# Three late stores of a decode-attention backward kernel go by rows in steps of 2, 4 and 8, and two small outputs leave in smaller pieces

## The chip, the cores and the metric

The kernel runs on one core of one Trainium2 chip. The metric is the device time of one execution in microseconds (us), the median of three runs. The profile is one further execution taken with the hardware profiler; its span runs from the first to the last instruction, and every position "at 714.57" in this text is in us from the start of that span.

## What is computed

The reference is one decode step (one token) of a transformer block, attention over a cache beside a gated MLP, and its gradients:

```python
def _A_ref(x, k_cache, v_cache, wq, wo):          # 32 heads, 8192 keys, head size 128
    q = (x @ wq).reshape(B, Sq, Hq, Dh).transpose(0, 2, 1, 3)
    scores = jnp.einsum("bhqd,bhkd->bhqk", q, k) * (Dh ** -0.5)
    p = _softmax(scores, axis=-1)
    o = jnp.einsum("bhqk,bhkd->bhqd", p, v)
    return o.transpose(0, 2, 1, 3).reshape(B, Sq, Hq * Dh) @ wo

def _B_ref(x, w1, w3, w2):
    h = _silu(x @ w1) * (x @ w3)
    return h @ w2

xn = _layernorm(A_x)
out = A_x + _A_ref(xn, ...) + _B_ref(xn, ...)
# returned: out, and the gradients of A_x, k_cache, v_cache, wq, wo, w1, w3, w2 for a given grad_out
```

All tensors are bf16. The two caches are 32 heads x 8192 x 128, which is 2 MB for each head; they are read once, and their gradients, of the same size, are written once. That is 64 loads and 64 stores of 2 MB. out_0 is the output row (640 numbers), out_1 the gradient of the input row (640 numbers), out_2 and out_3 the gradients of the K and V caches.

## The kernel before, where the change touches it

K and V of a head are loaded into one of ten buffers as 128 partitions (rows) of 16 KB each. The gradient of the head is written over the loaded data in place, and the buffer is stored from there. All these loads and stores go through one function, which issues them from SyncE in the order of the calls:

```python
dkc = out_2.rearrange("b h (p j) d -> (b h) p (j d)", p=P)     # P = 128
dvc = out_3.rearrange("b h (p j) d -> (b h) p (j d)", p=P)
...
def fifo(out_, in_):
    nc.sync.dma_start(out_, in_)
...
def load_next():
    if not pending or len(free_slots) < lag[0]:
        return
    kind, h = pending.pop(0)
    t = free_slots.pop(0)
    fifo(t[:], (kc if kind == "K" else vc)[h])
    kv_tiles[(kind, h)] = t
...
def store(kind, h):
    t = kv_tiles.pop((kind, h))
    if kind == "K":
        hd.pop(h)
    fifo((dkc if kind == "K" else dvc)[h], t[:])
    free_slots.append(t)
    load_next()
```

The gradients are outer products on VectorE (line 466). They and the stores run one head behind the forward part; the last head is finished after the loop, and the last weight gradients follow:

```python
def outers_a(h):
    outer_v(h, 0, J // 2)
    outer_v(h, J // 2, J)
    store("V", h)
    outer_k(h, 0, J // 2)

def outers_b(h):
    outer_k(h, J // 2, J)
    store("K", h)
...
outers_a(H - 1)                      # H = 32
outers_b(H - 1)
fin_od(NG - 1)
fin_pe(NG - 1)
fin_wo(NG - 1)                       # store of the wo gradient, issued from GpSimd
for ci in range(NC):
    fin_wq(NG - 1, ci)               # store of the wq gradient, issued from GpSimd
...
nc.vector.tensor_copy(row_bf, acc[:, 0:DHALF])
out_0v = out_0.rearrange("a b (e c) -> (a b e) c", e=2)
for e in range(2):
    nc.scalar.dma_start(out_0v[e:e + 1, :], row_bf[64 * e:64 * e + 1, :])
...                                  # layernorm gradient, some 10 small instructions
nc.vector.tensor_copy(fin_bf[:], ps_o[0:NC, 0:P])          # NC = 5
nc.scalar.dma_start(out_1.rearrange("a b (c p) -> (a b c) p", p=P), fin_bf[:])
```

The order of the last stores is therefore V29, K29, V30, K30, V31, K31 (heads count from 0). The tile framework gives each transfer issued from SyncE or ScalarE one of eight completion semaphores[...].

Of the kernel before, what the change touches and what calls it, by code (L numbers as in the profile page):

```python
# [16 lines left out]
P = 128  # L17
# [4 lines left out]
def kernel(  # L22
# [22 lines left out]
    nc = tc.nc  # L45
    H = A_k_cache.shape[1]
# [5 lines left out]
    NC = D // P  # L52
# [23 lines left out]
    dkc = out_2.rearrange("b h (p j) d -> (b h) p (j d)", p=P)  # L76
    dvc = out_3.rearrange("b h (p j) d -> (b h) p (j d)", p=P)
# [26 lines left out]
    def fifo(out_, in_):  # L104
        nc.sync.dma_start(out_, in_)
# [16 lines left out]
# [7 lines that stand above are left out]
# [84 lines left out]
    def t_tile():  # L213
        t = kt_tile()
        return t[:].rearrange("p k w -> p (k w)").bitcast(BF16)
# [248 lines left out]
    def outer(dst, vec, pair, lo, hi):  # L464
        n = hi - lo
        nc.vector.tensor_tensor(  # L466
            dst[:, lo * DH:hi * DH].rearrange("p (j a b) -> p j a b", a=DH // 2, b=2),
            vec.rearrange("p (a b) -> p a b", b=2).unsqueeze(1).to_broadcast([P, n, DH // 2, 2]),
            pair[:, lo:hi, :].unsqueeze(2).to_broadcast([P, n, DH // 2, 2]), ALU.mult)
# [4 lines left out]
    def outer_k(h, lo, hi):  # L474
        outer(kv_tiles[("K", h)], hd[h]["qd"][:, 0, :], hd[h]["U2"], lo, hi)

    def store(kind, h):
        t = kv_tiles.pop((kind, h))
        if kind == "K":
            hd.pop(h)  # L480
        fifo((dkc if kind == "K" else dvc)[h], t[:])
        free_slots.append(t)
        load_next()

# [236 lines left out]
# [9 lines that stand above are left out]
# [102 lines left out]
    nc.vector.tensor_tensor(dxn[:], dxn[:], dxm[:], ALU.add)  # L832
    row_bf = t_tile()[:, 0:DHALF]
    nc.vector.tensor_copy(row_bf, acc[:, 0:DHALF])
    out_0v = out_0.rearrange("a b (e c) -> (a b e) c", e=2)
    for e in range(2):
        nc.scalar.dma_start(out_0v[e:e + 1, :], row_bf[64 * e:64 * e + 1, :])
    st = consts.tile([P, 2], F32, name="st")
    nc.vector.tensor_reduce(st[:, 0:1], dxn[:], AX.X, ALU.add)
    junk5 = consts.tile([P, NC], F32, name="junk5")  # L840
# [10 lines left out]
    nc.tensor.transpose(ps_o[0:NC, 0:P], fin[:], ident_f[:])  # L851
    fin_bf = consts.tile([NC, P], BF16, name="fin_bf")
    nc.vector.tensor_copy(fin_bf[:], ps_o[0:NC, 0:P])
    nc.scalar.dma_start(out_1.rearrange("a b (c p) -> (a b c) p", p=P), fin_bf[:])


# [28 lines left out]
```

## Time and profile before

| what | value |
|---|---|
| time, median of 3 | 732.62 us (732.5 to 733.53) |
| profiled span | 731.1 us |
| moved by DMA | 303.53 MB, mean 415 GB/s |
| stores of K and V gradients | 64 of 2048 KB, 31.0 us from issue to landing |
| loads of K and V | 64 of 2048 KB, 26.3 us from issue to landing |
| TensorE, VectorE, ScalarE busy | 82%, 63%, 51% of the span |
| last load (V31) issued, landed | 660.35, 686.66 |
| last outer product (K31) ends | 706.1 |
| out_0 issued, out_1 issued | 714.57, 717.24 |

A line of the grouped views reads: source line, engine, operation, output<-input, count, then busy time. In a line of the timeline the first number is the start, the second how long it took. SPq and ACTq are the queues in which SyncE and ScalarE issue transfers. In the table by stage each row is one stretch of time with the busy time of every engine, the clock of TensorE, the mean busy share of the 16 DMA engines and the rate that they moved.

### The profile page before, as it was taken

The page shows a single profiled execution, that of the slowest core. Times are in us where ns is not written, and L with a number is a line of the kernel's source. Part 1 is how long each engine was busy: PE and PEld are TensorE (multiplying, and loading weights), DVE is VectorE, ACT ScalarE, POOL GpSimd, SP SyncE. Part 2 cuts the span into 40 slices and gives each one's busy share as a digit, 9 for nine tenths or more (in the row PEclk, how much of TensorE's full clock was granted, in tenths as well). Part 3 has the DMA queues.
Part 4 walks back from the last instruction along what each step waited for, and adds up shares of the span by engine and source line. Part 5 has one row for each costly group of instructions (what it writes and reads, how often), then busy time and mean ns, then how long its engine had stood idle before and what let it go on. Part 6 is the DMA issues. An engine that isn't in the chain of part 4 may idle for free.

```text
span 731.1 us, 12909 instructions
## 1 busy us (share of the span) xinstructions
PE 602.7 (82%) x5193; PEld 376.1 (51%) x5193; DVE 461.3 (63%) x811; ACT 375.8 (51%) x727; POOL 29.9 (4%) x45
## 2 busy tenths in 40 slices
PE   3989589999999989886987898789697879977930
PEld 2557356665566556554555554455464545544510
DVE  4179646677768886676546765647656775667581
ACT  3640736665666566554554554545464545555510
POOL 0010100000100000001000000000000000000000
PEclk9996799999999999999998999989999999999965
DMA  8999999999999999999999999999999999999993
GB/s 344 403 410 422 424 429 426 418 421 424 422 407 428 428 425 424 425 428 431 423 430 425 431 424 428 427 430 426 426 428 427 430 425 429 429 429 430 430 407 130
DMA packets 27135, 303.53 MB, mean 415 GB/s; under 512 B 2798, under 2 KB 4146, under 8 KB 10434
## 3 DMA queue, kind: packets, MB, share of 16 engines
q1 hardware_dynamic: 21328, 276.39, 89.4%
q0 software_dynamic: 5728, 26.30, 8.9%
q8 instruction: 41, 0.67, 0.4%
q14 instruction: 20, 0.16, 0.1%
q10 hardware_dynamic: 18, 0.01, 0.0%
HBM read 151.34 MB, written 151.34 MB: 414 GB/s over the span
## 4 chain that ended last, share of the span: by engine, by line
DMA 51%; PE 35%; DVE 6%; ACT 3%; issue 1%; SPq 0%; ACTq 0%; DVEq 0%
DMA kv<-in_A_k_cache_dram 22%; DMA out_dram<-kv 17%; PE pT L318 16%; DMA kv<-in_A_v_cache_dram 11%; PE sA L339 4%; PE dA L339 3%; PE X L433 3%; DVE kv L466 3%; PE m L356 2%; DMA wo_g<-in_A_wo_dram 2%; ACT KT L320 1%; ACT kv L630 1%; PE gu_ps L549 1%; PE dh_ps L560 1%; PE dx_acc L648 1%
## 5 line engine op out<-in xcount | busy, mean ns | idle before, releaser
L320 ACT COPY KT<-pT 128x512 f32<-128x512 f32 x512 | 288.0, 587 | 229.5 <-PE pT L318 209.0
L318 PE MATMUL pT<-ident_f,kv 128*128 128x128 f32 x2048 | 308.2, 290 | 60.3 <-DMA kv<-in_A_v_cache_dram 29.5
L318 PEld LDWEIGHTS pT<-ident_f,kv 128*128 128x128 f32 x2048 | 237.1, 149 | 153.7 <-issue 52.2
L466 DVE TENSOR_TENSOR kv<-qd,U 128x4096 bf16<-128x4096 bf16 x64 | 146.1, 2285 | 0.0
L466 DVE TENSOR_TENSOR kv<-qd,P 128x4096 bf16<-128x4096 bf16 x64 | 143.6, 2285 | 0.0
L433 PE MATMUL X<-kv,Z 128*32 128x512 bf16 x1024 | 94.3, 405 | 1.8 <-DVE Z L450 1.8
L339 PE MATMUL sA<-KT,qz 128*32 128x512 bf16 x512 | 83.9, 408 | 0.0
L339 PE MATMUL dA<-KT,qz 128*32 128x512 bf16 x512 | 83.8, 406 | 0.0
L416 DVE SCALAR_TENSOR_TENSOR U<-m,P 128x64 bf16<-128x64 f32 x32 | 7.5, 234 | 82.0 <-PE m L356 82.0
L382 DVE TENSOR_REDUCE mrow<-m 128x1 f32<-128x64 f32 x32 | 7.2, 223 | 75.3 <-PE m L356 75.2
L339 PEld LDWEIGHTS <-qz 128*32 128x32 bf16 x1024 | 29.5, 95 | 40.9 <-issue 38.3
L433 PEld LDWEIGHTS <-Z 128*32 128x32 bf16 x1024 | 32.5, 99 | 34.5 <-issue 6.9
L356 PE MATMUL m<-selc,KT 64*128 64x64 f32 x256 | 30.2, 240 | 8.1 <-ACT KT L346 7.9
L356 PEld LDWEIGHTS m<-selc,KT 64*128 64x128 f32 x256 | 21.3, 142 | 30.1 <-ACT KT L346 21.2
L376 ACT CAST qd<-pT 128x256 bf16<-128x256 f32 x32 | 11.9, 372 | 41.1 <-DVE kv L466 31.6
L389 DVE TENSOR_REDUCE negM<-m 128x1 f32<-128x128 f32 x32 | 9.3, 292 | 33.3 <-PE m L386 33.3
L514 DVE SCALAR_TENSOR_TENSOR wq_g<-wq_g,side 128x512 bf16<-128x512 bf16 x40 | 27.3, 683 | 0.0
L257 DVE SCALAR_TENSOR_TENSOR side<-wo_g,g_bc 128x640 bf16<-128x640 bf16 x32 | 26.2, 820 | 1.1 <-DMA wo_g<-in_A_wo_dram 0.7
L448 DVE SCALAR_TENSOR_TENSOR U<-m,P 128x128 bf16<-128x128 f32 x32 | 11.4, 355 | 15.7 <-PE m L446 15.7
L406 DVE RECIPROCAL rZ<-m 128x1 f32<-128x1 f32 x32 | 5.3, 167 | 24.1 <-PE m L400 24.1
L346 ACT COPY KT<-dA 64x512 f32<-64x512 f32 x32 | 18.6, 583 | 3.1 <-PE dA L339 3.1
L346 ACT COPY KT<-sA 64x512 f32<-64x512 f32 x32 | 18.6, 580 | 2.3 <-PE sA L339 1.9
(161 smaller groups left out, 373.3 us busy)
## 6 DMA issues: line engine op xcount, KB each, us to landing
out_dram<-kv SPq DMA_DIRECT2D x64, 2048.0 KB, 31.0
kv<-in_A_k_cache_dram SPq DMA_DIRECT2D x32, 2048.0 KB, 26.3
kv<-in_A_v_cache_dram SPq DMA_DIRECT2D x32, 2048.0 KB, 26.3
out_dram<-wo_g POOLq DMA_DIRECT2D x8, 640.0 KB, 11.5
out_dram<-wq_g POOLq DMA_DIRECT2D x8, 640.0 KB, 13.3
wq_g<-in_A_wq_dram POOLq DMA_DIRECT2D x7, 640.0 KB, 13.3
wo_g<-in_A_wo_dram POOLq DMA_DIRECT2D x7, 640.0 KB, 19.1
kv<-in_B_w_dram SPq DMA_DIRECT2D x2, 1728.0 KB, 27.9
```

Source lines behind the costliest of these rows:

```text
L257: nc.vector.scalar_tensor_tensor(junk[:], G_["wo"][:, hh, :], 1.0, g_bc[:], ALU.mult, ALU.mult, accum_out=G_["do"][:, hh:hh + 1])
L318: nc.tensor.transpose(pT[:, k * P:(k + 1) * P], W3[:, 4 * c + k, :], ident_f[:])
L320: nc.scalar.copy(KT[:].rearrange("p k w -> p (k w)"), pT[:])
L339: nc.tensor.matmul(S_[kind][q:q + QW, :], lhsT=S_["qz"][:, o:o + QW], rhs=KTb[c][:, par, :], start=(c0 == 0 and par == 0), stop=(c0 == NCH ...
L346: nc.scalar.copy(XS[0:QH].rearrange("p k w -> p (k w)"), S_.pop(kind)[0:QH, :])
L356: nc.tensor.matmul(S_["m"][:, b0:b0 + 4 * J].rearrange("p (x c k t) -> p k x c t", x=4, k=4, t=2)[:, k], lhsT=XS[0:QH, k, :], rhs=selc[0:Q ...
L376: nc.scalar.copy(qd[:].rearrange("p a d -> p (a d)"), hd[h].pop("ps_r"))
L389: nc.vector.tensor_reduce(S_["negM"][:], S_["m"][:, 2 * J:2 * J + P], AX.X, ALU.max, negate=True)
L433: nc.tensor.matmul(xg["X"][q:q + QW, :], lhsT=Z[:, o:o + QW], rhs=W[:, N4 * i:N4 * (i + 1)], start=(slot == 0 and i < 4), stop=(slot == NS ...
L448: nc.vector.scalar_tensor_tensor(S_["U2"][:], S_["V"][:, 0:J].unsqueeze(2).to_broadcast([P, J, 2]), S_["m"][:, OC + NS:OC + NS + 1], S_["P ...
L466: nc.vector.tensor_tensor(dst[:, lo * DH:hi * DH].rearrange("p (j a b) -> p j a b", a=DH // 2, b=2), vec.rearrange("p (a b) -> p a b", b=2 ...
L514: nc.vector.scalar_tensor_tensor(wq_g[:, ci, :], wq_g[:, ci, :], 1.0, dqb, ALU.mult, ALU.mult, accum_out=dxa[:, ci, g:g + 1])
```

## The change

Each of the stores of V29, K29 and V30 is cut by rows into seven transfers: every second row (64 rows), every fourth from row 1 (32 rows), every eighth from row 3 (16 rows), and the remaining 16 rows, every eighth from row 7, as four transfers of four rows. [...] the aim is to take some rows off most engines and to give them to a few, and to keep the two small outputs on the same few.

```diff
+    SPLIT = {("V", H - 3), ("K", H - 3), ("V", H - 2)}
+
     def store(kind, h):
         t = kv_tiles.pop((kind, h))
         if kind == "K":
             hd.pop(h)
-        fifo((dkc if kind == "K" else dvc)[h], t[:])
+        dst = (dkc if kind == "K" else dvc)[h]
+        if (kind, h) in SPLIT:
+            for i, st_ in ((0, 2), (1, 4), (3, 8)):
+                fifo(dst[i:P:st_], t[i:P:st_])
+            for b in range(4):
+                rs = slice(7 + 32 * b, 32 * (b + 1), 8)
+                fifo(dst[rs], t[rs])
+        else:
+            fifo(dst, t[:])
         free_slots.append(t)
         load_next()
...
-    out_0v = out_0.rearrange("a b (e c) -> (a b e) c", e=2)
+    out_0v = out_0.rearrange("a b (e q c) -> (a b e) q c", e=2, q=4)
     for e in range(2):
-        nc.scalar.dma_start(out_0v[e:e + 1, :], row_bf[64 * e:64 * e + 1, :])
+        nc.scalar.dma_start(out_0v[e:e + 1], row_bf[64 * e:64 * e + 1, :].rearrange("p (q c) -> p q c", q=4))
...
-    nc.scalar.dma_start(out_1.rearrange("a b (c p) -> (a b c) p", p=P), fin_bf[:])
+    for lo, hi in ((0, 4), (4, NC)):
+        nc.scalar.dma_start(out_1.rearrange("a b (c p) -> (a b c) p", p=P)[lo:hi, :], fin_bf[lo:hi, :])
```

## The prediction

> **What bounds the kernel now.** I read the page from its second part down, then the last 30 us: the busy table by stage, SyncE's and ScalarE's issues in order of time, SyncE's waits. The page says that the 16 DMA engines are full nearly throughout:
>
> ```profile
> DMA  8999999999999999999999999999999999999993
> ...
> HBM read 151.34 MB, written 151.34 MB: 414 GB/s over the span
> ```
>
> Only the last slice (18.3 us) falls, to 3 tenths. The change touches nothing before the last three heads, so the tail is what has to be read. The table by stage (us, busy time of the five engines, clock, DMA share, GB/s):
>
> ```profile
> 660.00:700.00 40.00, 33.05 (x288) 19.41 (x278) 25.90 (x35) 19.49 (x39) 0.86 (x1) 0.96 1.00 425
> 700.00:710.00 10.00, 2.16 (x15) 1.14 (x14) 8.85 (x13) 0.75 (x2) 0.77 (x1) 0.50 0.97 410
> ...
> 715.00:720.00 5.00, 0.76 (x3) 0.38 (x3) 1.12 (x5) 0.00 (x0) 0.00 (x0) 0.50 0.67 268
> 720.00:725.00 5.00, 0.00 (x0) 0.00 (x0) 0.00 (x0) 0.00 (x0) 0.00 (x0) 0.50 0.07 30
> 725.00:729.80 4.80, 0.00 (x0) 0.00 (x0) 0.00 (x0) 0.00 (x0) 0.00 (x0) 0.50 0.06 26
> ```
>
> From 720 on no compute engine works and the DMA share is 0.06 to 0.07, which is one engine of sixteen (0.0625) at 26 to 30 GB/s. The packet records say the same: fifteen engines run out by about 720.5, one goes on alone to 729.7, and the span ends 1.4 us later. Its last packets are rows of the last stores. A row of 16 KB takes 611 ns in the records, which is also 16,384 B over 429/16 GB/s.
>
> SyncE issues the last eight stores in this order (start, duration, count); ScalarE then sends out_0 (two issues) and out_1:
>
> ```profile
> 660.72 3.59 SPq L105 DMA_DIRECT2D out_dram<-kv  x3
> ...
> 674.53 0.33 SPq L105 DMA_DIRECT2D out_dram<-kv  x1
> ...
> 685.43 21.07 SPq L105 DMA_DIRECT2D out_dram<-kv  x4
> ...
> 714.57 0.55 ACTq L837 DMA_DIRECT2D out_dram<-KT  x2
> ...
> 717.24 0.27 ACTq L854 DMA_DIRECT2D out_dram<-fin_bf  x1
> ```
>
> By the code's order these are V28, K28, V29; K29; V30, K30, V31, K31. The last load (V31) is issued just before them, at 660.35. All stores are thus queued by 706.5, some 23 us before the queue is empty: the tail is a backlog in the DMA queue, and SyncE's waits after 704 are only the closing ones:
>
> ```profile
> SPq L880 <- DMA out_dram<-wq_g: 12.0, 1, 12.0
> SPq L880 <- DMA out_dram<-KT: 9.1, 1, 9.1
> SPq L105 <- DVE od_bf L491: 3.8, 1, 3.8
> SPq L880 <- DMA out_dram<-kv: 2.2, 1, 2.2
> ```
>
> The 9.1 us for out_0 (tile KT) end between 706.5 + 9.1 = 715.6 and 731.1 - 0.7 - 2.2 - 12.0 = 716.2 (0.7 us go to PE's sequencer at the very end), so about 716.0 is when its landing is seen by a waiting queue.
>
> [...] out_1's five rows leave as five packets of 256 B, out_0's single rows as one packet of 640 B each. One of out_1's five packets rides on the late engine and out_0's do not[...]
>
> **The change part by part.**
>
> *Rows.* In each of V29, K29, V30 the transfers of 64, 32 and 16 rows give every engine 4 + 2 + 1 = 7 rows; the four transfers of four rows give engines 0 to 3 four more, so 11. Over three stores engines 4 to 15 lose 3 rows (3 x 0.611 = 1.8 us), engines 0 to 3 gain 9 (5.5 us). If the late engine is 4, and nothing else changes, it ends at 727.9 and engines 0 to 3 at about 726: the intended gain is 1.8 us, and 732.6 becomes 730.8.
>
> *Issues.* SyncE has 18 more (21 for 3), at 0.33 to 0.5 us each some 8 us of a queue that mostly sleeps. By itself nothing.
>
> *out_0.* In the built program its access is merged back to one run of 320 elements, as before: no change. out_1 becomes two transfers (four rows, one row).
>
> *Semaphores: what I expect to decide it.* In the built program the transfers of SyncE and ScalarE take eight completion semaphores in turn, each adding 16, and an issue waits until the previous user of its semaphore is complete. The turns are handed out in the scheduler's order, and there out_0 and out_1 come before the late stores. Before, they hold turns that no later store needs: the waits of K30, V31, K31 are on V28, K28 and V29 (and loads). After, the extra transfers push the stores round the ring. V29's four-row transfers wait for K28 and for V29's own pieces, which is harmless. But the 64 rows of K29 are on semaphore 0 and wait for 288; the load of K31 brings it to 272, and the only other user that can supply the missing 16 is the first half of out_0. K29's 32 rows wait for the second half, its 16 rows and its first four-row transfer for the two pieces of out_1. SyncE issues in order, so K29, V30, K30, V31 and K31, five stores or 10.5 MB, stand still until out_0 has landed at the end of the compute chain.
>
> Working: out_0 is issued at 714.57 as before (VectorE depends on no late store) and is seen at about 716.0. K29's first rows move 0.8 us after issue (out_1: issued 717.24, packets at 718.04), so at 716.8. Engines 0 to 3 then have 11 + 11 + 8 + 8 + 8 = 46 rows, 46 x 0.611 = 28.1 us; the other engines 38 rows, 23.2 us. The wq store, issued at 714.13, still has about half of its 10 x 0.16 us per engine: 0.8 us. Engines 0 to 3 thus end at 716.8 + 28.1 + 0.8 = 745.7, the others at 740.8. I followed the chain of waits with these numbers and 0.6 us per landing: V30's pieces wait for K29's, K30 for K29's last four-row transfer (about 725), V31 and K31 for V30's 64 and 32 rows, and engines 0 to 3 always have rows queued, so the waits make no further hole. With 1.4 us at the end the span is 747.1, which is 16.0 us more than 731.1: 748.6. [...] I choose 1.5 us: **750 us**, 2.4% slower.
>
> **The rivals.** (1) The intended balance, 730.8: for it speaks the lone engine after 720; against it the wait on out_0, which is in the program. (2) The wait holds, but the four-row transfers are spread over other engines: then each has about 40 rows, 24.4 us, and the end is near 742, so 745. [...] (3) Without the wait, the late engine is 1, 2 or 3 and gets 5.5 us more: 738. [...]
>
> **Range and chances.** The hold until out_0 and the 10.5 MB behind it are nearly certain to me, so I give 3% to (1) and (3) together. [...] 745.5 to 756.5. The 2% line is 747.3[...]; hence 0.8 for slower, 0.19 for the same, 0.01 for faster.
>
> **What would show it.** In the changed profile SyncE should wait, at the split stores, some 20 to 25 us for out_0 (tile KT), with V29's pieces the only stores issued between 664 and 716; the DMA share should be near zero from about 693 to 716 but for wo and wq; then about 24 us near 1.0 and some 5 us at 0.25, four engines. The compute lines should end at 717.2 as before. A share of 0.06 at the end would say that the late engine matters still. The prediction is wrong if K29's first piece is issued near 674.5; too high if the last phase has no step at 0.25, too low if rows there take clearly over 611 ns.

## The result and the profile after

The changed kernel takes **754.25 us** (median of 5 runs, 753.3 to 755.37), the kernel before beside it 732.5 us (730.29 to 733.53). The ratio is 1.030 (95% interval 1.028 to 1.032): slower, by 21.75 us. The profiled spans are 753.5 and 731.1 us.

The page of the changed kernel, its row of DMA load (40 slices, now of 18.8 us each) and its bytes:

```profile
DMA  9999999999999999999999999999999999995168
...
HBM read 151.34 MB, written 151.34 MB: 402 GB/s over the span
```

The same bytes have moved at a lower mean rate. Slices 37 and 38 (678 to 716) fall to 5 and 1 tenths, where before there was no gap. The table by stage of the changed kernel, with the columns explained above, opens these slices:

```profile
690.00:700.00 10.00, 8.54 (x82) 4.60 (x80) 5.70 (x11) 4.70 (x10) 0.00 (x0) 1.00 0.09 36
700.00:710.00 10.00, 3.69 (x20) 2.66 (x20) 8.88 (x11) 0.99 (x3) 0.00 (x0) 0.51 0.06 22
...
716.00:722.40 6.40, 0.86 (x3) 0.49 (x3) 1.12 (x5) 0.00 (x0) 0.09 (x1) 0.50 0.88 350
722.40:724.50 2.10, 0.00 (x0) 0.00 (x0) 0.00 (x0) 0.00 (x0) 0.00 (x0) 0.50 0.00 0
724.50:727.50 3.00, 0.00 (x0) 0.00 (x0) 0.00 (x0) 0.00 (x0) 0.00 (x0) 0.50 0.56 153
727.50:732.00 4.50, 0.00 (x0) 0.00 (x0) 0.00 (x0) 0.00 (x0) 0.00 (x0) 0.50 1.01 379
732.00:735.00 3.00, 0.00 (x0) 0.00 (x0) 0.00 (x0) 0.00 (x0) 0.00 (x0) 0.50 0.32 120
735.00:750.00 15.00, 0.00 (x0) 0.00 (x0) 0.00 (x0) 0.00 (x0) 0.00 (x0) 0.50 1.00 418
750.00:752.00 2.00, 0.00 (x0) 0.00 (x0) 0.00 (x0) 0.00 (x0) 0.00 (x0) 0.50 0.14 57
```

Before, 700 to 710 ran at a share of 0.97. Now it runs at 0.06, although gradients lie ready in their buffers. After 716 there are 36 us of stores, and they have holes: nothing at all moves from 722.4 to 724.5, and the share is 0.56 at 724.5 to 727.5 and 0.32 at 732 to 735.

Who stands still, and for what, is in SyncE's waits of the changed kernel (total us, times, longest us):

```profile
SPq L105 <- DMA out_dram<-kv: 52.8, 6, 26.1
SPq L105 <- DMA out_dram<-KT: 15.2, 2, 15.0
SPq L891 <- DMA out_dram<-kv: 15.0, 1, 15.0
SPq L105 <- DMA out_dram<-fin_bf: 5.2, 1, 5.2
```

Line 105 is the function that issues loads and stores, so a store of a cache gradient waited 15.0 us for out_0 (tile KT), and another 5.2 us for out_1 (tile fin_bf). No data connects them; they share completion semaphores. The built program has every transfer add 16 to its semaphore (in the trace of before, five of the eight got 272 updates from 17 transfers or 288 from 18, 16 each). In the trace of the changed kernel the landings of out_0's first half and of K29's 64 rows are on one semaphore, and so are those of its second half and K29's 32 rows, of out_1's four rows and K29's 16 rows, and of out_1's last row and K29's first four-row transfer. The order in time is in the timeline of SyncE and ScalarE (start, duration, count):

```profile
660.24 10.06 SPq L105 DMA_DIRECT2D out_dram<-kv  x5
669.77 0.53 SPq L105 DMA_DIRECT2D out_dram<-kv  x1
696.38 0.72 SPq L105 DMA_DIRECT2D out_dram<-kv  x1
...
715.67 0.55 ACTq L847 DMA_DIRECT2D out_dram<-KT  x2
716.84 0.52 SPq L105 DMA_DIRECT2D out_dram<-kv  x1
717.60 0.49 SPq L105 DMA_DIRECT2D out_dram<-kv  x1
718.34 1.33 ACTq L865 DMA_DIRECT2D out_dram<-fin_bf  x2
723.32 3.09 SPq L105 DMA_DIRECT2D out_dram<-kv  x5
...
734.19 0.38 SPq L105 DMA_DIRECT2D out_dram<-kv  x1
```

Of the K and V stores, only V29's four four-row transfers go out between 670.3 and 716 (the first at 696.38, after 26.1 us of waiting for K28). K29's 64 rows follow out_0 by 1.2 us. K29's 16 rows go at 723.32, after out_1, and with them its four-row transfers. From there the trace shows no further wait of SyncE for a landing: fifteen issues follow each other, at 0.4 to 1.8 us each. K30 is reached only at 734.19, and the last three stores (K30, V31, K31: 24 rows on every engine) then fill 735 to 750.

Over how many engines a piece goes can be read from the landings in the same trace. Each of the nine pieces of 64, 32 and 16 rows updates its semaphore 16 times (K29's 64 rows from 721.38 to 722.09). Each of the twelve four-row transfers gives one update and then four: K29's first, issued at 723.90, at 724.93 and at 726.96 to 727.04. By the packet records only four engines carry rows from about 726.0 to 727.7, one after the other those of K29's four-row transfers: these share the same four. No record numbers the engines; that four-row transfers go to engines 0 to 3 was the author's assumption. They are called the four below.

### The profile page after: what moved, and what is told of

Read it like the earlier page. It is cut to its first block, busy times and chain, and to the rows that moved or that the text cites. A ratio compares the mean times of both kernels' runs of the same rounds, so it can differ in the third digit from the quotient of the medians.

```text
span 753.5 us, 12928 instructions
## 1 busy us (share of the span) xinstructions
PE 598.3 (79%) x5193; PEld 375.0 (50%) x5193; DVE 461.1 (61%) x811; ACT 375.4 (50%) x727; POOL 29.9 (4%) x45
## 4 chain that ended last, share of the span: by engine, by line
DMA 50%; PE 35%; DVE 6%; ACT 2%; issue 1%; SPq 0%; ACTq 0%; DVEq 0%
DMA out_dram<-kv 24%; PE pT L318 16%; DMA kv<-in_A_k_cache_dram 14%; DMA kv<-in_A_v_cache_dram 10%; PE sA L339 5%; PE dA L339 3%; PE X L433 3%; DVE kv L466 3%; PE m L356 2%; DMA wo_g<-in_A_wo_dram 2%; ACT KT L320 1%; PE gu_ps L559 1%; ACT KT L346 1%; PE m L400 0%; DVE side L257 0%
```

## The experiments

The theory: the extra transfers push late stores round the ring of eight semaphores onto out_0 and out_1, and this hold makes the time. The rival: it is the pieces themselves (slower rows, more rows on the four engines, more issues), with the wait only seen beside them. Each experiment was compared with the kernel before on the same chip, where that took 731.8 to 732.1 us.

### The small outputs taken off the ring

The changed kernel, with out_0 and out_1 issued from GpSimd, whose transfers do not use these eight semaphores. All splits stay.

```diff
-        nc.scalar.dma_start(out_0v[e:e + 1], ...)
+        nc.gpsimd.dma_start(out_0v[e:e + 1], ...)
...
-        nc.scalar.dma_start(out_1.rearrange("a b (c p) -> (a b c) p", p=P)[lo:hi, :], fin_bf[lo:hi, :])
+        nc.gpsimd.dma_start(out_1.rearrange("a b (c p) -> (a b c) p", p=P)[lo:hi, :], fin_bf[lo:hi, :])
```

> The changed kernel with its three split stores, but out_0 and out_1 issued from GpSimd, whose transfers use other semaphores; the late stores then wait only for stores and loads eight transfers back. Theory (the hold on out_0 makes the loss): K29's 64 rows are issued near 696, once K28 has landed, instead of at 716.9, and the time is 733 to 738 us; engines 0 to 3 carry 46 rows and end last. Rival (the pieces and the 46 rows make the loss, wherever they start): 750 us or more.

It took 736.78 us, ratio 1.007 (1.005 to 1.009): of the 21.75 us over before, 17.1 are gone and 4.7 stay. The timeline shows K29's first piece 21 us earlier:

```profile
695.38 0.52 SPq L105 DMA_DIRECT2D out_dram<-kv  x1
```

and the table by stage shows the gap half filled:

```profile
690.00:700.00 10.00, 6.35 (x64) 3.61 (x64) 8.43 (x11) 2.83 (x8) 0.00 (x0) 0.97 0.50 206
700.00:710.00 10.00, 1.81 (x12) 0.88 (x12) 8.78 (x18) 0.59 (x1) 0.77 (x1) 0.50 0.81 274
```

Half only: what stays is the ring among the pieces themselves. K29's 64 rows now wait for K28, its 32 rows for V29's 64. The DMA engines run short at 690 to 700, and the pieces cost 4.7 us even without the small outputs. The rival alone (750 or more) is out.

### The hold without the pieces

The kernel before, unsplit. K29 and the four stores after it are placed behind out_0, and a copy of two columns of K29's buffer onto themselves, on VectorE after out_0, holds them until then. The stores' order and rows are as before.

```diff
-        fifo((dkc if kind == "K" else dvc)[h], t[:])
+        dst = (dkc if kind == "K" else dvc)[h]
+        if h == H - 3 and kind == "K" or h > H - 3:
+            held.append((dst, t))
+        else:
+            fifo(dst, t[:])
...
+    first = held[0][1]
+    nc.vector.tensor_copy(first[:, 0:2], first[:, 0:2])
+    for dst, t in held:
+        fifo(dst, t[:])
```

> The kernel before, unsplit, but the stores of K29, V30, K30, V31, K31 come after out_0 in the program, and a copy of two columns of K29's buffer onto itself late in VectorE's chain (about 716.7) holds K29 and, by SyncE's order, the four behind it. Theory: five whole stores, 40 rows x 0.611 = 24.4 us from about 717.8, so an end near 742.5 and a time of 745 us (743 to 747); what the changed kernel has above that (9 us) belongs to its pieces. Rival (the hold costs little): 735 us or less.

It took 745.88 us, ratio 1.0187 (1.0170 to 1.0205), 13.8 us over before. Its table by stage has the same gap, and then an unbroken drain:

```profile
700.00:710.00 10.00, 1.81 (x12) 0.88 (x12) 8.81 (x16) 0.59 (x1) 0.77 (x1) 0.50 0.09 31
...
730.00:735.00 5.00, 0.00 (x0) 0.00 (x0) 0.00 (x0) 0.00 (x0) 0.00 (x0) 0.50 1.00 426
740.00:743.00 3.00, 0.00 (x0) 0.00 (x0) 0.00 (x0) 0.00 (x0) 0.00 (x0) 0.50 0.23 98
```

The last row ends at 741.5: 40 rows x 0.611 = 24.4 us after the issues at 714.55 and later leave 2.5 us for the start and the rest of wq. By the packet records all engines run out between about 740.9 and 741.5. The lone engine's 9.2 us at the end of the kernel before are gone: in the hold the engines had run nearly empty (share 0.09 at 700 to 710). That is why a gap of more than 20 us costs only 13.8. So the hold alone is worth 13.8 us, and the pieces, once held, another 8.0 (21.75 - 13.8). Unheld they cost 4.7 us (above): after the hold (share 0.06 at 700 to 710) the DMA engines have no other rows left to cover a wait of the pieces (read from the traces, not tried by itself).

### The small outputs alone

The kernel before with only the change to out_0 and out_1 (the second and third part of the diff above).

> The kernel before with the change of out_0 and out_1 alone. out_0 is merged back to one run, out_1 goes as four rows and one row; no late store waits for either. Theory: no difference, 732.5 us (within 0.3%). Rival (the smaller pieces of the outputs cost time themselves): 735 us or more.

It took 731.81 us, ratio 0.9998 (0.9989 to 1.0007). This part does nothing to the time by itself. It does move one landing: before, four of out_1's five packets move at 717.99 to 718.29 and the fifth only at 720.94, as soon as a row of the late engine ends. With four rows and one row apart, the last of the five goes at 718.33.

### One split store instead of three

```diff
-    SPLIT = {("V", H - 3), ("K", H - 3), ("V", H - 2)}
+    SPLIT = {("V", H - 2)}
```

> The changed kernel with only V30 split. By the semaphores V30's third four-row transfer waits for out_0 and K30's store for out_1, so three whole stores (24 rows, 14.7 us) start after out_1 has landed, near 719 to 720, instead of five. Theory: end near 735, time 737 to 739 us. Rival (the loss goes with the number of split stores, a third of 22 us): 739 to 740 us, but without a stop of SyncE until out_0; the view of SyncE's waits decides between them.

It took 737.3 us, ratio 1.0077 (1.0064 to 1.0091). With six extra transfers instead of 18, other stores fall on the small outputs. SyncE's waits:

```profile
SPq L105 <- DMA out_dram<-KT: 5.3, 2, 5.1
SPq L105 <- DMA out_dram<-fin_bf: 2.9, 1, 2.9
```

K30, V31 and K31 go out at 718.2 to 719.1. One split is enough to meet the outputs, with fewer stores behind the wait. The DMA share is 0.29 already at 700 to 705, before out_0 is issued (712.77), so part of the 5.5 us lost comes from the pieces' waits for older stores.

### The six extra rows on the four engines

The changed kernel, where the last 16 rows of each split store go as four transfers of 16 rows by a quarter of the columns (4 KB each) instead of four transfers of four whole rows. Transfers and waits are as many; each engine now has eight rows' worth, if 16 rows go over 16 engines as the 16-row pieces of the change do (16 updates each).

```diff
-                rs = slice(7 + 32 * b, 32 * (b + 1), 8)
-                fifo(dst[rs], t[rs])
+                cs = slice(KVN // 4 * b, KVN // 4 * (b + 1))
+                fifo(dst[7:P:8, cs], t[7:P:8, cs])
```

> The changed kernel, but the last sixteen rows of each split store go as four transfers of 16 rows and a quarter of the columns (4 KB) instead of four transfers of four rows: as many transfers, the same waits, but all 16 engines move 8 rows of every store. If the six extra rows on engines 0 to 3 (3.7 us) are part of what stands above the plain hold: 750 to 752 us. If only the hold, the wait on out_1 and the chain of issues count: 754 us. If the whole excess were the imbalance: 746 us.

It took 750.66 us, ratio 1.0257 (1.0243 to 1.0271), 18.8 us over the kernel before on its chip: 2.9 us less than the change. In the profiled runs out_0 came 1.4 us earlier here (its longest wait is 13.0 us instead of 15.0); from the end of that wait to the end of the span it is 34.2 us instead of 36.7, so 2.5 us are the rows'. Six rows were counted at 6 x 0.611 = 3.7 us. Part of the difference shows in this run's packet records: after 724 there are five short holes, 0.9 us together, in which no engine moves anything.

### Contiguous rows

The changed kernel with the first two pieces contiguous (rows 0 to 63, 64 to 95) and the last 32 rows in the same numbers as before.

```diff
-            for i, st_ in ((0, 2), (1, 4), (3, 8)):
-                fifo(dst[i:P:st_], t[i:P:st_])
+            for rs in (slice(0, 64), slice(64, 96), slice(96, P, 2)):
+                fifo(dst[rs], t[rs])
             for b in range(4):
-                rs = slice(7 + 32 * b, 32 * (b + 1), 8)
+                rs = slice(97 + 2 * b, P, 8)
```

> The changed kernel with rows 0 to 63, then rows 64 to 95, as contiguous pieces instead of steps of 2 and 4; the remaining 32 rows again as 16 rows and four times four. [...] a row takes 1.2 us instead of 0.61: 6 rows x 0.6 us in each of K29 and V30, about 7 us more than the changed kernel, 760 to 763 us. If rows may lie anywhere: 754 us and rows at 611 ns.

It took 760.58 us, ratio 1.0383 (1.0367 to 1.0398): 28.8 us over the kernel before on its chip, 7.0 more than the change. Once the contiguous 64-row piece of K29 is under way, its 16-KB rows take 1,269 to 1,281 ns in the packet records; in the change, 95 of the 96 rows of K29's 64- and 32-row pieces take 611 to 650 ns (the other 719), as an unsplit store's rows do. So the strides of the change cost those two pieces nothing. K29's 16-row piece, though, takes 944 to 1,492 ns a row (mean about 1.2 us). So 64 rows by two and 32 by four ran at 611 to 650 ns, 16 rows by eight and 64 in sequence at about twice that; the records do not show why.

### The same split in mid-run, and as late as possible

Two tries to get the intended balance without the small outputs. In the first, the seven-piece split is on V of heads 9, 14, 19 and 24 of the kernel before, and the late stores are whole.

```diff
+    SPLIT = {("V", h) for h in (9, 14, 19, 24)}
```

> The same split into seven transfers, but of four stores in mid-run (V of heads 9, 14, 19, 24); late stores, out_0 and out_1 as before, so nothing is held. If each split takes one row (0.611 us) off the engine that ends last: 732.5 - 2.4 = 730 us. If the 16-row piece takes twice the time per row [...] (1.1 to 1.4 us a row in the changed kernel's packet records), the gain is cancelled: 732.5 us. If the ring of eight semaphores starves the queue during each split: 735 us or more.

It took 735.0 us, ratio 1.0045 (1.0029 to 1.0060). The lone engine's tail is much shorter, as its table by stage shows:

```profile
720.00:725.00 5.00, 0.00 (x0) 0.00 (x0) 0.00 (x0) 0.00 (x0) 0.00 (x0) 0.50 1.00 422
725.00:732.00 7.00, 0.00 (x0) 0.00 (x0) 0.00 (x0) 0.00 (x0) 0.00 (x0) 0.50 0.33 139
```

But the three stretches of 100 us from 300 to 600 moved 416, 419 and 423 GB/s, against 428, 428 and 427 before, and each split held SyncE up (V9's pieces go from 251.3 to 272.7, the next load at 279.6, where the rhythm is some 10 us). So the other engines end later too: at 726.5 eleven still carry rows, where before only one did. Four rows are 2.4 us, and the shorter tail is not their doing alone. How much of the loss is the ring and how much the slow rows of the 16-row pieces is not separated.

In the second, only the very last store K31 is split: 64 rows, 32 rows, eight transfers of four rows.

```diff
+        if (kind, h) == ("K", H - 1):
+            for i, st_ in ((0, 2), (1, 4)):
+                fifo(dst[i:P:st_], t[i:P:st_])
+            for b in range(8):
+                rs = slice(3 + 16 * b, 16 * (b + 1), 4)
+                fifo(dst[rs], t[rs])
```

> The kernel before, out_0 and out_1 as before, with only the very last store (K31) split: 64 rows in steps of 2, 32 in steps of 4, and the last 32 rows as eight four-row transfers, no 16-row piece. Nothing stands behind it in the queue and its pieces wait only for older stores and for out_0 and out_1, which land before they are due. If the late engine is not among engines 0 to 3 it moves two rows less: 1.2 us off, 730.9 us (ratio 0.998). If it is one of 0 to 3: 6 rows more, 736 us.

It took 733.12 us, ratio 1.0018 (1.0011 to 1.0025), slower where 1.2 us less were expected. The late engine did end earlier (last row at about 727.6 instead of 729.7), but the last two four-row transfers had to wait for K31's own 64 and 32 rows. They were issued at 726.49 and 728.20, and they ended the program. Before that, SyncE had waited 5.3 us for out_1, which was expected to have landed in time.

### Four-row transfers behind the last store

The kernel before with only V31 split (64, 32, eight times four rows), its last seven four-row transfers issued behind K31, so that no whole store stands behind one that waits.

```diff
+        four = [slice(3 + 16 * b, 16 * (b + 1), 4) for b in range(8)]
+        if (kind, h) == ("V", H - 1):
+            fifo(dst[0:P:2], t[0:P:2])
+            fifo(dst[1:P:4], t[1:P:4])
+            fifo(dst[four[0]], t[four[0]])
+            late.extend((dst, t, rs) for rs in four[1:])
...
+        if (kind, h) == ("K", H - 1):
+            for d_, t_, rs in late:
+                fifo(d_[rs], t_[rs])
```

> The kernel before with V31 alone split: 64 rows in steps of 2, 32 in steps of 4, and 32 rows as eight four-row transfers, of which one goes ahead of K31's store and seven after it, so that no four-row transfer waits for K31 (in the run with K31 split the last two did, and ended the program). The late engine moves two rows less and the others have room. Theory: 1.2 us off, 730.6 us (ratio 0.998). Rival (extra transfers cost more than two rows are worth): 732 us or more.

It took **730.87 us, ratio 0.9984 (0.9978 to 0.9991)**, where the kernel before took 732.12: it beats both kernels, the kernel before by 1.2 us (0.7 to 1.6). Its table by stage has the lone engine's stretch filled and shortened, and the span ends at 729.4:

```profile
720.00:725.00 5.00, 0.00 (x0) 0.00 (x0) 0.00 (x0) 0.00 (x0) 0.00 (x0) 0.50 0.24 89
725.00:729.40 4.40, 0.00 (x0) 0.00 (x0) 0.00 (x0) 0.00 (x0) 0.00 (x0) 0.50 0.15 61
```

The four-row transfers do wait for the small outputs, as SyncE's waits show:

```profile
SPq L105 <- DMA out_dram<-KT: 8.0, 2, 6.7
...
SPq L105 <- DMA out_dram<-fin_bf: 1.2, 1, 1.2
```

Here that costs nothing that the time shows, because K31 had been issued at 711.68 and only these narrow transfers stand behind the waits.

Two rows fewer on 12 engines are 2 x 0.611 = 1.2 us; six rows more on the late engine would have cost 3.7. So the late engine is one of those twelve; no record says which. Together with the lone tail of the kernel before this is what the change was after.

Taking more of the same, K30 and V31 both split in this way (16 four-row transfers, 9 ahead of K31) and the small outputs issued from GpSimd:

> The same for K30 and V31, sixteen four-row transfers, nine of them ahead of K31's store, with out_0 and out_1 issued from GpSimd so that no store waits for them. Four rows less on the late engine, 2.4 us: 729.5 us if it never runs dry. But K31 waits for a four-row transfer that waits in turn for V31's pieces, so the late engine may stand idle before K31: then 732 to 735 us.

It took 736.77 us, ratio 1.0064 (1.0051 to 1.0076), worse than either reading allowed. SyncE's waits for earlier stores around the end of the computation:

```profile
SPq L105 <- DMA out_dram<-kv: 11.2, 6, 4.2
```

Six waits, 11.2 us. The table by stage of the same kernel:

```profile
710.00:715.00 5.00, 0.00 (x0) 0.00 (x0) 4.79 (x18) 0.00 (x0) 0.63 (x2) 0.50 0.44 161
715.00:720.00 5.00, 0.93 (x3) 0.58 (x3) 1.55 (x9) 0.00 (x0) 2.29 (x4) 0.50 0.50 175
```

K31 came out only at 721.93, behind the chain of nine four-row transfers, and meanwhile the engines ran at half. In this program a four-row transfer has to land before the eighth after it may go, and the longest of the six waits here is 4.2 us. In the changed kernel K29's four-row transfers landed 3.1 to 3.8 us after their issue, where a row takes 0.6.

Last, the three stores in pieces of 64, 32 and 32 rows (steps of 2, 4 and 4), with no four-row transfers, and the small outputs issued from GpSimd:

```diff
-            for i, st_ in ((0, 2), (1, 4), (3, 8)):
+            for i, st_ in ((0, 2), (1, 4), (3, 4)):
                 fifo(dst[i:P:st_], t[i:P:st_])
-            for b in range(4):
-                ...
```

> The three late stores in three pieces each (64 rows in steps of 2, 32 and 32 in steps of 4), eight rows on every engine, no 16-row and no four-row pieces, out_0 and out_1 from GpSimd. Theory: no wait for out_0, [...] nine transfers do not fill the ring of eight in a way that stops the queue: 732 us, the same as before. If cutting stores into strided pieces costs time as such: 734 us or more.

It took 733.25 us, ratio 1.0017 (1.0010 to 1.0023), 1.1 us over before: six extra transfers cost little when nothing late stands in the ring, but their DMA share at 690 to 700 is 0.72, not 1.00.

## Why the prediction was right, and where it was off

**The semaphores**, the deciding step, held as written. K29's 64 rows went out 1.2 us after out_0 was issued (at 716.84; about 716.0 was predicted), its 16 rows after out_1, and the five stores stood still. The DMA share of 0.06 to 0.09 from 690 to 710 is the predicted sign. The wait for out_0 itself is 15.0 us and not 20 to 25, because V29's four-row transfers had first waited for K28 and V29 until 701.2. The prediction called these harmless, and they are: the next issue was held until 716.84 anyway. Without the outputs in the ring 17.1 us are gone; the hold alone makes 13.8.

**The rows.** 40 rows x 0.611 us after the release and the predicted start (0.8 us after the issue, 0.8 us of wq) put the end of the unsplit, held stores at 740.6; it was 741.5. The six extra rows on the four engines, counted as 3.7 us, are worth 2.5 to 2.9. But the sign given for them, a step at 0.25 at the end, did not come: all engines end between 749.9 and 751.8. K30 stands behind V30's four-row transfers in SyncE's order, so the step came in the middle and in two parts. By the packet records only four engines carry rows from about 726.0 to 727.7 (K29's four-row transfers) and from 733.2 to 735.1 (V30's), 3.6 us together.

**The slow rows.** The 1.5 us on top of 748.6 were the author's estimate; no trace of before showed them. K29's 16-row piece does take twice the time, 0.6 us more on every engine; with V30's at the same rate it would be 1.2 us. The mean of all 16-KB rows after the release is 651 ns (617 in the run with the hold alone). Against 611 that is 40 x 0.040 = 1.6 us on an engine, so 1.5 was right in size. In place it was luck: the prediction added it to the four engines alone, but the twelve rows of K29's four-row transfers that can be told apart took 611 to 625 ns, and the slow 16-row pieces have a row on every engine. That strided pieces are slow as such is refuted by the 611 to 650 ns of K29's 64- and 32-row pieces and by what contiguous pieces cost (28.8 us over before, against 21.75).

**The step that was off** is "the waits make no further hole". The sum was 748.6 without slower rows; with 1.6 us for the slower rows it would be 750.2, and 754.25 was measured. Half of the missing 4 us is one hole. out_1's landing was taken as 0.8 us after its issue. In the kernel before, that is when four of its five packets move; the fifth moves 3.7 us after the issue (717.24 to 720.94), behind a row of the late engine, so the trace already had the warning. In the changed kernel out_1 was issued at 718.34, but all five packets moved only at 722.2 to 722.4, just when the rows of K29 that were queued by then had been moved. K29's 16 rows waited for them: 2.1 us with all engines idle. The run with contiguous rows fits this: where the rows ahead take twice as long, out_1's packets move 7.0 us after their issue (718.57 to 725.55), and the wait for it is 8.3 us instead of 5.2.

The issues were slower than assumed as well (0.4 to 1.8 us each against 0.33 to 0.5), and K30 came at 734.19 instead of about 725. The trace does not show that this moved the end. From 724.5 to 750.9 at least four engines carry rows at every moment, and K30's first rows (735.08) start as the last of V30's four-row transfers end. If these are the same four throughout, they never ran dry after the hole; the late K30 only let the other twelve stand idle, and all then ended together.

The remaining 2 us are not assigned: the engines end unevenly, and the profiled run lies 1 us above the median. In it out_0 came 1.1 us later than in the profile of before; over all profiled runs out_0 is issued between 712.8 and 716.7, so single profiles scatter by more than that. None of these parts was run by itself.

**The intended gain** (rival 1: 1.8 us if the late engine is outside the four) is real in kind: moving two rows off each of 12 engines brought 1.2 us once no whole store stood behind the waits. The 1.8 us of three rows were reached in no run.

The budget of the 21.75 us: the hold 13.8 (run), the extra rows about 2.9 (run), and about 5.1 left. Of these the trace gives 2.1 to the hole before out_1's landing and about 1.4 to slower rows (651 ns against 617 with the hold alone, 40 rows); some 1.6 us are not assigned.

**Open.** The cause of the late engine's lag was not tried; the run with V31 in four-row transfers (1.2 us faster, where 3.7 us would have been lost) only puts it outside the four that carry them. Why an issue of SyncE takes up to 1.8 us is open. Why the 16 rows by eight and the 64 contiguous rows take about twice the time is open, and so is what the mid-run split lost to slow rows and what to the ring.

## What to carry to other kernels

In a program that hands out completion semaphores in turn (eight here), a transfer cut into pieces takes as many turns as it has pieces, and a later transfer may then wait for something that has nothing to do with it (here 15.0 us for out_0). Before splitting late transfers, write down for each issue which earlier transfer has to have landed, and look for one that hangs on the end of the computation. Where a few engines are to take more rows, issue the narrow transfers last, behind the wide ones, and take strides whose rows the packet records show at the rate of an unsplit store (here 64 by two and 32 by four, 611 to 650 ns; not 16 by eight, about 1.2 us).

## What was not expected of the hardware

- Five packets of 256 B, issued from ScalarE while 16-KB rows from SyncE were queued, moved only 3.9 us after their issue (718.34 to 722.2), as those rows ended; in the run with contiguous pieces, where the rows took twice as long, 7.0 us. In the kernel before, four of the five took 0.8 us and the one on the late engine 3.7 us.
- The same 16-KB row of K29 takes 611 to 650 ns in pieces of 64 rows by two or 32 by four (once 719), about 1.2 us in 16 rows by eight, and about 1.27 us in 64 contiguous rows. Eight rows of the changed kernel that start between 727.89 and 728.14, after the first rows of V30, took 986 to 1,366 ns.
- SyncE's issue of one transfer took 0.3 to 0.5 us alone and up to 1.8 us in the chain of pieces. It is not the pieces alone: with the hold alone, five whole stores issued one after the other took 0.34 to 1.26 us each.
